# A weight decoder's last step: one VectorE pass for the low bits, where a VectorE shift and a GpSimd addition stood

## The chip, the core and the metric

The kernel runs on one core of a Trainium2 chip. The core has a tensor engine (TensorE, PE in the profile, with its weight loads as PEld), a vector engine (VectorE, DVE), a scalar engine (ScalarE, ACT), GpSimd (POOL), and a queue (SyncE, SP) that starts most of the transfers. The engines work through their own instructions in order and wait for each other by semaphores. The metric is the device time in microseconds, the median of the runs.

## What is computed

Attention of 4 sequences of 576 tokens with 8 heads of 64, half of the heads with a window of 32 tokens, half with a window of 128 in which only every fourth token counts; then two feed-forward layers over all 2304 tokens. The weights of the layers come in as float64.

```
x   = attention(q, k, v)                    # [2304, 512]
xn  = x / sqrt(mean(x * x) + 1e-6) * rms_g
g   = xn @ w_gate                           # [512, 1536]
x   = (silu(g) * (xn @ w_val)) @ w_out      # [1536, 512]
h   = x @ w_in                              # [512, 2048]
out = (max(h, 0) + alpha * min(h, 0)) @ w_out2
```

## The kernel before

**Operands.** Every operand of a large product is a pair of float16 numbers, hi and lo, of the operand times a power of two found on the chip; a product is hi·hi + hi·lo + lo·hi.

**Weights.** They come in 68 blocks of 128 x 512 numbers: gate, val and out of the 12 chunks of the first layer, then in and out of the 16 chunks of the second. On chip they live in `wb`, 70 slots of 2 KB a partition. A block takes two slots as it lands (float64, that is 512 pairs of int32 words), one as float32, one as hi and lo. A block goes through these steps:

- `load_w` (L195): a transfer of 512 KB, issued on SP.
- `decode_w` (L197 to L207): the float64 bits become float32 bits. L202 (VectorE) shifts the high word left by 3 and masks it; L203 (VectorE) puts the two top bits back, with a mask and an or; L204 (VectorE) shifts the low word right by 29, in place, which leaves 3 bits; L205 (GpSimd) adds them to the result as integers. The two landing slots are then free for another load.
- `norm_w`: Gram products on TensorE, or a square on ScalarE (L294), from which the power of two for a group of blocks follows through L256, L310, L313 and L318 to L321 on VectorE.
- `split_w` (L377 to L388): hi on ScalarE (L382); lo on VectorE (L387), or for every third or second block on ScalarE and GpSimd (L384, L385).

**Attention.** The first 128 tokens of the sequences and some later groups are done in float32 with slots of `wb` as their buffers: L585 loads, L595 turns, scores with L541 to L549, L621 turns, L556 to L561 weigh the values, L691 to L693 norm x, L705 to L707 turn it for the first layer.

**Order.** The Python code writes the work down in one sequence, in which the attention's steps, the decoding (`pump`) and the products of the layers are interleaved by a planner that counts slots and products, not time. From that sequence a scheduler with a timeline of its own sorts the instructions of each engine; each engine then works through its list in that order.

Of the kernel before, what the change touches and what calls it, by code (L numbers as in the profile page):

```python
# [22 lines left out]
# Every operand of a large product is carried as a pair of float16 numbers, hi + lo, of the  # L23
# operand times a power of two that is found on the chip so that nothing overflows; a product
# is hi*hi + hi*lo + lo*hi, accumulated in float32, and the powers of two are taken out again.
# The weights come as the bits of float64 numbers and are made float32 on the chip.
# [3 lines left out]
def kernel(  # L30
# [54 lines left out]
    # q: hi, lo, lo, hi and k: hi, lo of each head; rows that a group has no query for hold old ones  # L85
# [27 lines left out]
    def band(m, rows, cols, c0, lo, hi, off=0):  # L113
        # keeps m[p, c0 + c] where lo <= c - (p - off) <= hi
        view = m[0:rows, c0:c0 + cols]
        nc.gpsimd.affine_select(
            out=view, in_=view, compare_op=ALU.is_ge, fill=NEG,
            base=off - lo, pattern=[[1, cols]], channel_multiplier=-1,
        )
        nc.gpsimd.affine_select(  # L120
            out=view, in_=view, compare_op=ALU.is_ge, fill=NEG,
            base=hi - off, pattern=[[-1, cols]], channel_multiplier=1,
        )

    def constants():
        nc.vector.memset(ident, 0.0)
        nc.gpsimd.affine_select(
            out=ident, in_=ident, compare_op=ALU.not_equal, fill=1.0,
            base=0, pattern=[[-1, 128]], channel_multiplier=1,
        )  # L130
        nc.vector.memset(ones_1, 1.0)
        nc.vector.memset(eps, 1e-30)
        nc.gpsimd.memset(qkhl, 0.0)
        nc.vector.memset(mhalf, -0.5)
        for m in (m_spp, m_norm, m_tail):
            nc.vector.memset(m, BIG)
        band(m_spp, 128, 128, 0, -31, 0)
        # m_spd: 0 <= p - c and p % 4 == c % 4
        et = wk.tile([4, 32, 4], BF16, tag="st", bufs=2, name="et")
        nc.vector.memset(et, 0.0)  # L140
        nc.gpsimd.affine_select(
            out=et, in_=et, compare_op=ALU.not_equal, fill=1.0,
            base=0, pattern=[[0, 32], [-1, 4]], channel_multiplier=1,
        )
        same = psw()[:, 0:128]
        mm(same, et.rearrange("p a c -> p (a c)"), et.rearrange("p a c -> p (a c)"), True, True)
        nc.vector.tensor_scalar(m_spd, same, BIG, NEG, ALU.mult, ALU.add)
        band(m_spd, 128, 128, 0, -127, 0)
        band(m_norm, 96, 128, 0, 1, 32)
        for r in range(2):  # L150
            view = m_tail[:, 48 * r:48 * r + 48]
            band(m_tail, 32, 48, 48 * r, 1, 32, 16 * r)
            nc.gpsimd.affine_select(
                out=view, in_=view, compare_op=ALU.is_ge, fill=NEG,
                base=-16 if r else 15, pattern=[[0, 48]], channel_multiplier=1 if r else -1,
            )

# [1 line left out]
    # A block (512 numbers a partition) is two slots of 2 KB as it comes, one as float32 and  # L159
    # one as hi | lo.  # L160
# [12 lines left out]
    def one_slot():  # L173
        # the one that has been free for the longest
        i = min((i for i in range(NSLOT) if free[i]), key=lambda i: (given_back[i], i))
        free[i] = False
        return i
# [19 lines left out]
    def decode_w(b):  # L197
# [6 lines left out]
        nc.vector.tensor_scalar(r[:, :, 0], r[:, :, 0], 29, None, ALU.logical_shift_right)  # L204
        nc.gpsimd.tensor_tensor(w, w, r[:, :, 0], ALU.add)  # L205
# [18 lines left out]
    # Bounds of the squares of the columns' norms: the largest entry of W^T W (bfloat16 heads of  # L224
    # the entries). The scales of gate and val are those of a few blocks each, as the first
    # products begin before all of the weights are there; out's scales take the differences out.
# [18 lines left out]
    def gram(blocks, sums, dst):  # L245
        # blocks of [k, f]: each one's own columns, or the sums over all of them
# [35 lines left out]
    def norm_w(b):  # L282
# [7 lines left out]
        else:  # L290
            # sums of squares, on the engine that waits least then
# [14 lines left out]
    def over_partitions(src, n, dst):  # L306
        # the largest of the partitions' src[:, i], on every partition
# [7 lines left out]
    def root_scale(p, sg, rc):  # L315
        # p: bounds of squares. sg = 2^n with sqrt(p) sg < 2^15; rc = 1 / sg
        ri, si = rc.bitcast(I32), sg.bitcast(I32)
        nc.vector.tensor_scalar(ri, p.bitcast(I32), 1, EXPO, ALU.logical_shift_right, ALU.bitwise_and)  # L318
        nc.vector.tensor_scalar(si, ri, EXPO, None, ALU.bitwise_xor)
        nc.vector.tensor_scalar(sg, sg, 2.0 ** -51, None, ALU.mult)  # L320
        nc.vector.tensor_scalar(rc, rc, 2.0 ** 50, None, ALU.mult)  # L321

    # scales: gate and val of each chunk, out of each, in2, out2
# [9 lines left out]
    def scale_g():  # L333
        # sx with |x / rms * g| sx < 2^15, as |x / rms| <= sqrt(512)
# [8 lines left out]
    def scale_wo():  # L343
        # S with |out| S / (gate's scale * val's) < 2^15 in every chunk
# [12 lines left out]
        # what the last products carry: 2^-60 / (1/sx^2 * 1/S * 1/si * 1/sp)  # L357
# [33 lines left out]
    # The first 128 tokens of the sequences, the next 384 of each, and what is left of them.  # L391
# [61 lines left out]
    # the groups up to this one are float32 products  # L453
# [32 lines left out]
    def a_split_hi(i):  # L486
# [9 lines left out]
        # sc: 0:3 the scales of q, k, v; 3:6 their inverses by 2^50; 6 that of the scores  # L496
# [37 lines left out]
    def softmax(g, scores, scale):  # L534
        # scores: (in PSUM, their heads); leaves exp(s - max) in g["s"] and its sums in g["dn"]
# [16 lines left out]
    def weigh(g, ps, scale):  # L552
        # ps: the weighted values; x = ps / (sum + 1e-9)
# [14 lines left out]
    # The first 128 tokens of the sequences: float32 products, as the tensor engine waits for  # L568
    # weights then; the tiles are slots of the weights that are not yet there.
# [34 lines left out]
    def f_score(i):  # L604
        g = groups[i]
        nq, nk, qk = g["nq"], g["nk"], g["qk"]
        # products of different rows of the array go to different banks
# [108 lines left out]
    # Steps: (what goes before the products of a slot, block or None)  # L716
# [268 lines left out]
    # by when the steps up to the n-th have to be out  # L985
# [4 lines left out]
    def take(d):  # L990
        """The attention's steps that go with this slot."""
# [26 lines left out]
    def pump(n):  # L1018
        # n blocks of weights made float32, and loads of more
# [46 lines left out]
    # the first block's attention, and the weights of the first products as they come  # L1066
# [72 lines left out]
```

## Time and profile before

| | |
|---|---|
| median of 3 runs | 1027.07 us (1027.04 to 1027.49) |
| span of the profiled execution | 1026.5 us |
| TensorE busy | 937.2 us, 91% of the span |
| VectorE busy | 575.6 us, 56% |
| ScalarE busy | 559.9 us, 55% |
| GpSimd busy | 377.8 us, 37% |
| GpSimd's additions of L205 | 68, 100.3 us |

The shares are means over stages that differ: the weights are loaded and decoded in the first 300 us, and the rest of the run is products with what is then on chip. So the rows below are cut by stretches of time. A busy engine may be one whose instruction is held up; for that the length of an instruction is compared with that of its like elsewhere.

### The profile page before, as it was taken

Reading aid. Unit: us, or ns where it says so; the run is one execution under the profiler, and the core shown is the slowest. Engines: PE = TensorE matmul, PEld = TensorE weight load, DVE = VectorE, ACT = ScalarE, POOL = GpSimd, SP = SyncE. Lnnn points to the kernel's source line nnn. Section 1 sums busy time; section 2 is a strip of 40 time slices with the busy share of each in tenths; the row PEclk is TensorE's granted clock in tenths of the full one; section 3 lists DMA queues with packets and bytes.
Section 4 is the critical chain, followed back from the end, with each engine's and each line's share of the span. In section 5 each row is a group of like instructions: output and inputs, shape, how many; then the busy total and the mean of one; then the engine's idle time right before and its main releaser. Section 6 shows DMA issues by size and latency. Waiting matters only on the chain.

```text
span 1026.5 us, 17830 instructions
## 1 busy us (share of the span) xinstructions
PE 937.2 (91%) x6270; PEld 583.3 (57%) x6270; DVE 575.6 (56%) x1396; ACT 559.9 (55%) x1604; POOL 377.8 (37%) x394
## 2 busy tenths in 40 slices
PE   5454879988889989999999999999999999999997
PEld 3444765566545656665555555555555555765564
DVE  5999986787888766564445575434352111331111
ACT  3142657554669988777655677644454312333343
POOL 3564645345534454533232333322142211122222
PEclk9676889999899999999999999999999999999999
DMA  9991323643454354344344353331120000101000
GB/s 255 299 338 45 101 72 102 160 118 102 146 110 96 64 96 93 80 97 99 67 106 64 85 117 80 79 84 38 38 43 6 29 16 1 32 1 21 1 31 21
DMA packets 191608, 88.06 MB, mean 86 GB/s; under 512 B 176800, under 2 KB 180384, under 8 KB 191520
## 3 DMA queue, kind: packets, MB, share of 16 engines
q1 hardware_dynamic: 188896, 82.22, 33.0%
q10 hardware_dynamic: 2624, 4.72, 1.4%
q8 instruction: 49, 0.80, 0.3%
q14 instruction: 39, 0.32, 0.1%
HBM read 55.32 MB, written 6.55 MB: 60 GB/s over the span
## 4 chain that ended last, share of the span: by engine, by line
PE 68%; DVE 18%; DMA 6%; ACT 4%; issue 2%; POOL 1%; SPq 1%; ACTq 0%; DVEq 0%; POOLq 0%
PE psw L92 40%; PE acc L92 27%; DVE wb L203 3%; DVE wb L204 3%; DVE wb L202 2%; DMA wb<-in_moe_w_in_dram 2%; DVE wb L387 2%; DMA wb<-in_moe_w_out_dram 1%; DVE wb L693 1%; DVE wb L541 1%; DMA rkv<-in_v_dram 1%; DMA qkT<-qkhl 1%; DVE dn L556 1%; ACT wb L549 1%; POOL wb L205 1%
## 5 line engine op out<-in xcount | busy, mean ns | idle before, releaser
L92 PE MATMUL psw<-xy,wb 128*128 128x384 f16 (+1 forms) x3360 | 530.3, 307 | 5.2 <-DVE t L875 2.7
L92 PEld LDWEIGHTS <-wb 128*128 128x128 f16 (+1 forms) x4014 | 390.4, 100 | 247.5 <-issue 13.4
L92 PE MATMUL acc<-wb,hl 128*128 128x512 f16 x1002 | 246.2, 381 | 4.9 <-ACT hl L877 1.2
L932 DVE SCALAR_TENSOR_TENSOR p<-m,nal,p 128x384 f32<-128x384 f32 (+1 forms) x112 | 71.4, 638 | 166.6 <-ACT p L931 166.0
L92 PEld LDWEIGHTS <-hl 128*128 128x128 f16 x1002 | 96.0, 98 | 98.8 <-issue 3.4
L205 POOL TENSOR_TENSOR wb<-wb 128x512 int32<-128x512 int32 x68 | 100.3, 1482 | 94.5 <-DVE wb L203 61.8
L92 PE MATMUL acc<-wb 128*128 128x512 f16 x510 | 124.0, 379 | 0.7 <-ACT wb L934 0.6
L883 POOL TENSOR_TENSOR hl<-p,hl 128x384 f16<-128x384 f32 (+1 forms) x74 | 61.3, 828 | 116.4 <-ACT hl L934 103.9
L883 POOL TENSOR_TENSOR hl<-t,hl 128x384 f16<-128x384 f32 (+1 forms) x56 | 51.1, 912 | 129.6 <-ACT hl L877 129.6
L874 DVE SCALAR_TENSOR_TENSOR t<-t,psw 128x384 f32<-128x384 f32 (+1 forms) x84 | 41.2, 490 | 79.9 <-ACT t L873 79.7
L930 ACT ACTIVATE m<-psw 128x384 f32<-128x384 f32 (+1 forms) x112 | 48.6, 434 | 65.9 <-PE psw L92 65.1
L873 ACT ACTIVATE t<-psw,tsc 128x384 f32<-128x384 f32 (+1 forms) x84 | 44.1, 525 | 71.9 <-PE psw L92 62.7
L92 PE MATMUL psw<-wb 128*128 128x128 bf16 (+6 forms) x448 | 57.3, 301 | 10.7 <-POOL wb L205 8.4
L659 POOL TENSOR_TENSOR phl<-s,phl 96x512 f16<-96x512 f32 (+2 forms) x33 | 36.8, 1114 | 70.0 <-ACT phl L653 40.5
L382 ACT ACTIVATE wb<-wb,wsg 128x512 f16<-128x512 f32 x68 | 46.6, 711 | 27.3 <-DVE wrc L321 18.7
L875 DVE SCALAR_TENSOR_TENSOR t<-t,psw 128x384 f32<-128x384 f32 (+1 forms) x84 | 41.2, 490 | 27.8 <-PE psw L92 26.5
L549 ACT ACTIVATE s<-s,mx 96x128 f32<-96x128 f32 (+2 forms) x132 | 50.1, 381 | 10.9 <-DVE mx L546 10.7
L883 POOL TENSOR_TENSOR wb<-p,wb 128x384 f16<-128x384 f32 (+1 forms) x38 | 32.0, 842 | 63.5 <-ACT wb L934 57.5
L203 DVE SCALAR_TENSOR_TENSOR wb<-wb 128x512 int32<-128x512 int32 x68 | 54.7, 810 | 0.2
L883 POOL TENSOR_TENSOR wb<-t,wb 128x256 f16<-128x256 f32 (+1 forms) x28 | 24.1, 861 | 80.2 <-ACT wb L877 72.1
L877 ACT ACTIVATE hl<-t 128x384 f16<-128x384 f32 (+1 forms) x56 | 26.8, 479 | 44.4 <-DVE t L875 44.4
L934 ACT ACTIVATE hl<-p 128x384 f16<-128x384 f32 (+1 forms) x74 | 34.6, 467 | 28.9 <-DVE p L932 28.8
(160 smaller groups left out, 1154.2 us busy)
## 6 DMA issues: line engine op xcount, KB each, us to landing
wb<-in_moe_w_out_dram SPq DMA_DIRECT2D x28, 512.0 KB, 4.4
wb<-in_moe_w_in_dram SPq DMA_DIRECT2D x16, 512.0 KB, 3.6
wb<-in_moe_w_gate_dram SPq DMA_DIRECT2D x12, 512.0 KB, 7.7
wb<-in_moe_w_val_dram SPq DMA_DIRECT2D x12, 512.0 KB, 7.3
out_dram<-o ACTq DMA_DIRECT2D x16, 256.0 KB, 2.5
rkv<-in_k_dram SPq DMA_DIRECT2D x23, 128.0 KB, 2.7
rkv<-in_v_dram SPq DMA_DIRECT2D x23, 128.0 KB, 2.8
rq<-in_q_dram SPq DMA_DIRECT2D x23, 96.0 KB, 2.1
```

Source lines behind the costliest of these rows:

```text
L92: nc.tensor.matmul(o, a, b, start=start, stop=stop)
L203: nc.vector.scalar_tensor_tensor(w, r[:, :, 1], -0x40000000, w, ALU.bitwise_and, ALU.bitwise_or)
L205: nc.gpsimd.tensor_tensor(w, w, r[:, :, 0], ALU.add)
L382: nc.scalar.activation(half(b, 0), dec(b), ACTF.Copy, scale=wsg[:, s:s + 1])
L549: nc.scalar.activation(s[:nq, h, :nk], s[:nq, h, :nk], ACTF.Exp, bias=mx[:nq, 1, h:h + 1], accum_out=g["dn"][:nq, h])
L659: nc.gpsimd.tensor_tensor(phl[:nq, 1, :, :nk], g["s"][:nq, :, :nk], phl[:nq, 0, :, :nk], ALU.subtract)
L873: nc.scalar.activation(t[:, :T], pg[:, :T], ACTF.Tanh, scale=tsc[:, chunk(c):chunk(c) + 1])
L874: nc.vector.scalar_tensor_tensor(t[:, :T], t[:, :T], 1.0, pg[:, :T], ALU.add, ALU.mult)
L875: nc.vector.scalar_tensor_tensor(t[:, :T], t[:, :T], 2.0 ** -46, pv[:, :T], ALU.mult, ALU.mult)
L883: nc.gpsimd.tensor_tensor(a[:, 1, :T], t[:, :T], a[:, 0, :T], ALU.subtract)
L930: nc.scalar.activation(m[:, :T], ps[:, :T], ACTF.Relu, scale=-(2.0 ** -15))
L932: nc.vector.scalar_tensor_tensor(p[:, :T], m[:, :T], nal[:, c:c + 1], p[:, :T], ALU.mult, ALU.add)
```

## The change

L204 and L205 become one VectorE instruction that shifts the low word right by 29 and puts the result into `w` with an or (the three low bits of `w` are zero then, so or and plus are the same). The low word is no longer written back. The diff also takes comments out; the lines keep their numbers up to 203, and what follows `decode_w` stands one line higher: L541 is L540, L693 is L692, L707 is L706.

```diff
         nc.vector.tensor_scalar(w, r[:, :, 1], 3, 0x3FFFFFFF, ALU.logical_shift_left, ALU.bitwise_and)
         nc.vector.scalar_tensor_tensor(w, r[:, :, 1], -0x40000000, w, ALU.bitwise_and, ALU.bitwise_or)
-        nc.vector.tensor_scalar(r[:, :, 0], r[:, :, 0], 29, None, ALU.logical_shift_right)
-        nc.gpsimd.tensor_tensor(w, w, r[:, :, 0], ALU.add)
+        nc.vector.scalar_tensor_tensor(w, r[:, :, 0], 29, w, ALU.logical_shift_right, ALU.bitwise_or)
         give(i, i + 1)
```

The scheduler sorts all engines anew for it. VectorE's list at its first decoded blocks, before:

```order
L202 TENSOR_SCALAR wb<-wb 128x512
L204 TENSOR_SCALAR wb<-wb 128x512
L203 SCALAR_TENSOR_TENSOR wb<-wb 128x512
L147 TENSOR_SCALAR m_spd<-psw 128x128
L202 TENSOR_SCALAR wb<-wb 128x512
L204 TENSOR_SCALAR wb<-wb 128x512
L203 SCALAR_TENSOR_TENSOR wb<-wb 128x512
```

The same place now:

```order
L202 TENSOR_SCALAR wb<-wb 128x512
L203 SCALAR_TENSOR_TENSOR wb<-wb 128x512
L147 TENSOR_SCALAR m_spd<-psw 128x128
L204 SCALAR_TENSOR_TENSOR wb<-wb 128x512
L202 TENSOR_SCALAR wb<-wb 128x512
L203 SCALAR_TENSOR_TENSOR wb<-wb 128x512
L204 SCALAR_TENSOR_TENSOR wb<-wb 128x512
```

The number of VectorE instructions is the same; the third of a block comes last now and has two tensor inputs. On the same engine, where the first scales are there (`wsg`), the second group's x is normed (`ms` and `gs` are its inputs) and turned (`xy_73` is the first layer's input), and the first blocks are split, before:

```order
L280 TENSOR_SCALAR tsc<-xsc,wrc 128x1
L204 TENSOR_SCALAR wb<-wb 128x512
L387 SCALAR_TENSOR_TENSOR wb<-wb,wsg 128x512 x2
L693 SCALAR_TENSOR_TENSOR wb<-wb,ms,gs 128x512
L202 TENSOR_SCALAR wb<-wb 128x512
L387 SCALAR_TENSOR_TENSOR wb<-wb,wsg 128x512
L202 TENSOR_SCALAR wb<-wb 128x512
L387 SCALAR_TENSOR_TENSOR wb<-wb,wsg 128x512
L204 TENSOR_SCALAR wb<-wb 128x512
L203 SCALAR_TENSOR_TENSOR wb<-wb 128x512
L202 TENSOR_SCALAR wb<-wb 128x512
L203 SCALAR_TENSOR_TENSOR wb<-wb 128x512
```

and now:

```order
L279 TENSOR_SCALAR tsc<-xsc,wrc 128x1
L692 SCALAR_TENSOR_TENSOR wb<-wb,ms,gs 128x512
L204 SCALAR_TENSOR_TENSOR wb<-wb 128x512
L386 SCALAR_TENSOR_TENSOR wb<-wb,wsg 128x512 x2
L204 SCALAR_TENSOR_TENSOR wb<-wb 128x512
L386 SCALAR_TENSOR_TENSOR wb<-wb,wsg 128x512 x2
L202 TENSOR_SCALAR wb<-wb 128x512 x3
L706 TENSOR_TENSOR xy_73<-psw,xy_73 128x4x128
L202 TENSOR_SCALAR wb<-wb 128x512
L203 SCALAR_TENSOR_TENSOR wb<-wb 128x512 x3
```

The norm has moved ahead of the first splits, and the shifts of the next blocks stand together behind them. On GpSimd, around the last normed x of the float32 groups (`ms`), among the splits of the first layer's results (`hl`), before:

```order
L883 TENSOR_TENSOR hl_108<-t,hl_108 128x256
L205 TENSOR_TENSOR wb<-wb 128x512
L692 TENSOR_TENSOR ms<-ms,mhalf 96x1
L205 TENSOR_TENSOR wb<-wb 128x512 x3
L883 TENSOR_TENSOR hl_109<-t,hl_109 128x256
L205 TENSOR_TENSOR wb<-wb 128x512 x3
L883 TENSOR_TENSOR hl_110<-t,hl_110 128x256
```

and now:

```order
L691 TENSOR_TENSOR ms<-ms,mhalf 96x1
L882 TENSOR_TENSOR hl_110<-t,hl_110 128x256
L882 TENSOR_TENSOR hl_107<-t,hl_107 128x256
L882 TENSOR_TENSOR hl_108<-t,hl_108 128x256
L691 TENSOR_TENSOR ms<-ms,mhalf 96x1
L882 TENSOR_TENSOR hl_109<-t,hl_109 128x256
L882 TENSOR_TENSOR hl_110<-t,hl_110 128x256
```

The additions are gone and the rest keeps its order.

## Rows read from the trace of the kernel before

**Rows 1.** the page's slices (40 of 25.7 us, tenths of busy time): VectorE
```profile
DVE  5999986787888766564445575434352111331111
```

**Rows 2.** busy time by stretch (us; count), granted clock, DMA share, GB/s
```profile
25.00:61.00 36.00, 11.20 (x66) 10.47 (x67) 36.00 (x67) 9.97 (x24) 21.56 (x15) 0.64 0.98 314
61.00:135.00 74.00, 51.36 (x381) 42.75 (x381) 73.86 (x139) 31.96 (x81) 40.84 (x32) 0.78 0.38 130
135.00:300.00 165.00, 146.10 (x1027) 98.39 (x1028) 131.85 (x302) 98.87 (x311) 78.44 (x66) 0.94 0.45 121
300.00:1027.00 727.00, 714.10 (x4738) 422.77 (x4735) 320.29 (x845) 410.16 (x1158) 226.72 (x258) 1.00 0.27 56
```

**Rows 3.** chain of waits, 25 to 135 us, shares by line
```profile
by line: DVE wb L203 20.8%; DVE wb L204 19.4%; DVE wb L202 13.4%; DVE wb L387 12.5%; DVE dn L556 5.3%; DVE wb L693 4.2%; issue 3.7%; DVE nrm L256 3.5%; DVE wb L541 2.5%; DVE wb L561 2.2%; DVE t L874 2.1%; DVE mx L545 1.7%; DVE diag L310 1.6
```

**Rows 4.** TensorE's waits, 25 to 300 us: us in total, times, longest
```profile
PE psw L705 <- DVE wb L693: 28.6, 5, 15.6
PE psw L92 <- DVE diag L310: 15.2, 3, 8.4
PE psw L92 <- POOL wb L205: 8.4, 2, 6.2
```

**Rows 5.** groups, VectorE, 25 to 135 us (count, busy us, mean ns, idle)
```profile
L203 DVE SCALAR_TENSOR_TENSOR wb<-wb 128x512 int32<-128x512 int32 x30 | 25.5, 855 | 0.0
L204 DVE TENSOR_SCALAR wb<-wb 128x512 int32<-128x512 int32 x38 | 24.6, 650 | 0.0
L202 DVE TENSOR_SCALAR wb<-wb 128x512 int32<-128x512 int32 x30 | 18.1, 609 | 0.0
L387 DVE SCALAR_TENSOR_TENSOR wb<-wb,wsg 128x512 f16<-128x512 f32 x15 | 15.3, 1028 | 0.0
L556 DVE TENSOR_SCALAR dn<-dn 128x4 f32<-128x4 f32 x5 | 6.3, 1255 | 0.0
L693 DVE SCALAR_TENSOR_TENSOR wb<-wb,ms,gs 128x512 f32<-128x512 f32 x4 | 4.9, 1220 | 0.0
```

**Rows 6.** groups, VectorE, 0 to 25 us
```profile
L203 DVE SCALAR_TENSOR_TENSOR wb<-wb 128x512 int32<-128x512 int32 x4 | 2.7, 682 | 0.0
...
L204 DVE TENSOR_SCALAR wb<-wb 128x512 int32<-128x512 int32 x4 | 1.7, 428 | 0.0
...
L556 DVE TENSOR_SCALAR dn<-dn 128x4 f32<-128x4 f32 x3 | 0.5, 166 | 0.1
```

**Rows 7.** timeline, VectorE: start us, us, what
```profile
31.95 1.40 DVE L202 TENSOR_SCALAR wb<-wb 128x512 int32<-128x512 int32 x1
...
34.87 1.50 DVE L204 TENSOR_SCALAR wb<-wb 128x512 int32<-128x512 int32 x1
...
61.03 0.74 DVE L387 SCALAR_TENSOR_TENSOR wb<-wb,wsg 128x512 f16<-128x512 f32 x1
...
69.76 1.29 DVE L202 TENSOR_SCALAR wb<-wb 128x512 int32<-128x512 int32 x1
...
254.47 4.22 DVE L693 SCALAR_TENSOR_TENSOR wb<-wb,ms,gs 96x512 f32<-96x512 f32 x1 [1.34 <-POOL ms L692]
```

**Rows 8.** timeline, GpSimd
```profile
31.77 1.29 POOL L205 TENSOR_TENSOR wb<-wb 128x512 int32<-128x512 int32 x1 [0.63 <-DVE wb L203]
34.69 1.39 POOL L205 TENSOR_TENSOR wb<-wb 128x512 int32<-128x512 int32 x1 [1.63 <-DVE wb L203]
...
254.40 3.74 POOL L205 TENSOR_TENSOR wb<-wb 128x512 int32<-128x512 int32 x3
```

**Rows 9.** groups, GpSimd, 25 to 135 us
```profile
L205 POOL TENSOR_TENSOR wb<-wb 128x512 int32<-128x512 int32 x30 | 44.9, 1506 | 41.0 <-DVE wb L203 27.6 <-issue 6.7 <-ACT wb L384 4.3
```

**Rows 10.** timeline, SP
```profile
51.09 0.92 SPq L195 DMA_DIRECT2D wb<-in_moe_w_val_dram  x2
```

**Rows 11.** the page's transfers: count, KB, median us to landing
```profile
wb<-in_moe_w_val_dram SPq DMA_DIRECT2D x12, 512.0 KB, 7.3
```

**Rows 12.** chain of waits, 135 to 300 us, shares by line
```profile
by line: PE psw L92 17.5%; DMA wb<-in_moe_w_in_dram 10.1%; DMA wb<-in_moe_w_out_dram 7.6%; DVE wb L203 6.6%; issue 6.4%; DVE wb L202 5.9%; PE acc L92 5.3%; POOL wb L205 4.3%; DVE wb L693 3.4%; DVE wb L204 3.4%; DMA qkT<-qkhl 3.1%; ACT wb L5
```

## The prediction

> **What bounds the kernel now.** The page's slices come first [rows 1]: VectorE stands at 7 to 9 tenths from the second slice to the eighth and falls off slowly. Cut into stages [rows 2], the run has three. From 25 to 135 us (stage A) VectorE is busy 36.00 of 36 and 73.86 of 74 us, TensorE 11.20 and 51.36, at a mean granted clock of 0.64 and 0.78 of its full level. From 135 to 300 us (stage B) TensorE is busy 146.10 of 165 us and VectorE 131.85. After 300 us (stage C) TensorE is busy 714.10 of 727 us: what is late there is the products. The chain of waits in stage A [rows 3] is VectorE nearly throughout, and its three largest lines are the decoding of the weights: L203 20.8%, L204 19.4%, L202 13.4%. TensorE's waits up to 300 us are for VectorE's results (the normed x of L693, the diagonal of L310) and twice for the GpSimd addition itself [rows 4]. So stage A is worth what VectorE's queue is worth, microsecond for microsecond, as long as nothing else is late.
>
> Busy does not mean working there. The same lines have two lengths: before 25 us, where GpSimd and VectorE seldom meet, a shift of L204 takes 428 ns, a pass of L203 682 ns and the small L556 166 ns [rows 6]; from 25 to 135 us they take 650, 855 and 1255 ns on average [rows 5]. The timeline shows why [rows 7, 8]: the shift that begins at 31.95 takes 1.40 us and the one at 34.87 takes 1.50 us, and both last until just after the end of a GpSimd addition of L205, which began 0.18 us ahead of each (31.77 plus 1.29, 34.69 plus 1.39).
>
> **The change part by part.** Each of the 68 blocks loses one VectorE shift and one GpSimd addition and gets one VectorE pass with two tensor inputs.
>
> The new pass: the trace has no shift-and-or of this line, but L203 is the same operation on the same operands (a strided int32 input, w as second input and output, 512 elements), so I take its undisturbed 682 ns. Against the shift of 428 ns that is 0.254 us more a block [rows 6]. Stage A decodes 30 blocks (30 additions [rows 9], 30 of L203): 30 x 0.254 = 7.6 us more, all on VectorE's path. Bounds: 0 if the longer pass fills gaps (there are none, so I exclude it), and a doubled pass below, as a rival.
>
> The addition that goes: while it runs VectorE is held. Over the undisturbed lengths, stage A holds 30 x (855 - 682) = 5.2 us on L203, 38 x (650 - 428) = 8.4 on L204, 30 x (609 - 428) = 5.4 on L202, 5 x (1255 - 166) = 5.4 on L556, and against the 0.74 us of the row at 61.03 [rows 7] 15 x (1028 - 740) = 4.3 on L387 and 4 x (1220 - 740) = 1.9 on L693 [rows 5]: 30.6 us. Not all of it is L205's, since GpSimd also splits weights and activations then. L205 is 44.9 us [rows 9] of GpSimd's 21.56 + 40.84 = 62.4 us [rows 2], 72%, which gives 22 us. The upper end is all of it, 30.6 us, about 1.0 us for each of the 30 additions, and that is what the two pairs of [rows 7, 8] show (1.40 and 1.50 against about 0.42). I take 26 us, between them. Stage A: -26 + 7.6 = -18.4 us, with bounds of -22 + 7.6 = -14.4 and -30.6 + 7.6 = -23.0.
>
> The Trainium skill (SBUF — State Buffer, "Who interferes with whom") calls the port that VectorE and GpSimd share an exclusive lock: whoever starts first has it for its whole instruction, and the other is blocked, not slowed. By it an addition could cost VectorE up to its whole length of about 1.28 us, an estimate of 38 us for the 30; stage A would then be -31 us and the whole -36 us, 991 us. The rows stop at 30.6 us, as an addition often begins under an instruction that is already running.
>
> What could eat it in stage A is the loads. The 20th block's load is issued at 51.09 us; its first shift starts at 69.76 [rows 7, 10], and VectorE never waited for a load in this stage (idle 0.0 in [rows 5]). With a landing time of 7.3 us for such a block (the median of its like, [rows 11]) it is there by about 58.4, 11 us early. By then VectorE is ahead by some 18.4 x (70 - 25)/110 = 7.5 us. The cover holds with 3 or 4 us left. TensorE has 110 - 62.6 = 47 us of idle time in stage A to give.
>
> The order: the scheduler sorts anew. A block is now three passes in a row on VectorE where the addition went to the other queue, and the second normed x and its four first splits stand a few rows earlier. On TensorE 48 products of the first layer stand ahead of the second set of Gram products, before as after. So I price the order at nothing, with 3 us to either side in the range.
>
> Stage B: the decoding of the other 34 blocks. Here TensorE is the busiest, and the chain [rows 12] gives L205 4.3% of 165 us = 7.1 us and L204 3.4% = 5.6 us, which at stage A's mean of 650 ns [rows 5] is some 8.6 shifts, each 0.254 us longer: +2.2 us. Net -4.9 us. That is in keeping with the largest single wait: at 254.47 a normed x takes 4.22 us under three additions in a row [rows 7, 8], 3.5 us over 0.74, and TensorE's L705 stands behind it (a part of the 28.6 us of [rows 4]). Bounds: a gain of at most the 18.9 us that TensorE idles in the stage, and I go no further than -8; a loss of 34 x 0.254 = 8.6 us if every new pass were late and nothing came back, of which I keep 0 as the upper end, since the held time is seen here too. Stage C has no decoding: 0.
>
> **Sum.** -18.4 - 4.9 = -23.3 us. The profiled execution's span is 1026.5 us, 0.6 us under the median of 1027.07, so the median falls to about 1004 us.
>
> **The rivals.** (1) *Slower, because a full engine gets more work.* If the stretched lengths in stage A are not GpSimd's doing, or its other operations take the place that the additions leave, the new pass is a pure cost: +7.6 us in stage A and +2.2 in B, 1037 us. It decides when less than 7.6 of the 30.6 us goes away, 0.25 us an addition. Against it speak the ends of the stretched shifts, which follow the ends of the additions. For it the Trainium skill (Perfetto Trace Analysis, "Optimizing Scalar/DVE Operations") says that work may be taken off a saturated VectorE, to GpSimd too, though it adds that the two share a port, so that it might not help; here the first half would speak against this change, and the trace sides with the second.
> (2) *Something else is late.* Loads, TensorE at its lower clock (0.64 to 0.78 in stage A), or ScalarE takes over after half of stage A's gain, and stage B gives back nothing: -9 us, 1018 us. For it: the load cover is thin and the order of a few hundred instructions has moved. Against it: TensorE's 47 idle us.
> (3) *More*, if each addition holds VectorE for about its length, and the chain in stage B shortens by its upper end: -23 - 8 = -31 us, 996 us. The lock rule of the Trainium skill (SBUF — State Buffer), cited above, leans this way.
> (4) *The pass isn't what it seems.* If shift-and-or runs at half of L203's rate, 1.36 us, it costs 0.936 us over the shift: +28.1 - 26 = +2 us in stage A, and -7.1 + 8.0 = +0.9 in stage B, 1030 us. Nothing in the trace hints at it; L203 has a mask and an or, and the old L204 a shift, at the lengths of their kinds.
>
> **How the numbers follow.** Forecast 0.68, (1) 0.05, (2) 0.14, (3) 0.09, (4) 0.04. The forecast's own spread is -14.4 - 0 + 3 to -23 - 4.9 - 3, some 996 to 1016. Half of (2) and half of (3) are taken in for 8 in 10: 995 to 1018. A measurement of this kernel tells about 0.2%, 2 us, from no change. Faster 0.88 (the forecast, (3) and most of (2)), same 0.03 (a little of (2) and of the two bad cases), slower 0.09.
>
> **What would show it.** Right: from 25 us until the first layer runs freely VectorE's L202 and L203 near 0.43 and 0.69 us instead of 0.61 and 0.86; the new pass near 0.7; TensorE's long waits for L693 and L310 shorter, and the end of stage A at about 117 instead of 135 us; a span short by that and a little more. Wrong: the passes as long as before with GpSimd idle (1), VectorE idle before L202 for loads (2), or a new pass of over 1 us (4).

## The result, and the profile after

| | before | after |
|---|---|---|
| median | 1027.05 us (1025.52 to 1027.49) | 992.32 us (991.9 to 992.97) |
| ratio | | 0.9672, 95% interval 0.9658 to 0.9686 |
| span of the profiled execution | 1026.5 us | 990.8 us |
| TensorE busy | 937.2 us | 927.5 us |
| VectorE busy | 575.6 us | 546.4 us |
| GpSimd busy | 377.8 us | 285.9 us |

The change is a gain of 3.3%, 34.7 us of the median and 35.7 us of the span: in the foretold direction, but half as much again as the forecast's 23.3 us, and 2.7 us below the lower end of the range.

To see where it came from, the stages are cut by events instead of by the clock: stage A from 25 us to the end of the fourth normed x (L693 before, L692 after), stage B from there to the end of the last decoding pass (the last L203), stage C the rest. Up to 25 us the two traces are nearly alike. The columns of the first fence are those of [rows 2]; this is the kernel before by its own stage ends.

```profile
25.00:135.30 110.30, 62.56 (x446) 53.22 (x446) 110.16 (x206) 41.92 (x105) 62.39 (x47) 0.73 0.58 190
135.30:295.70 160.40, 141.80 (x1002) 96.04 (x1003) 128.86 (x295) 94.87 (x297) 75.16 (x63) 0.94 0.45 123
295.70:1026.50 730.80, 718.40 (x4763) 425.12 (x4761) 322.98 (x850) 414.17 (x1173) 230.00 (x261) 1.00 0.27 56
```

The same view of the changed kernel:

```profile
25.00:118.80 93.80, 58.78 (x451) 51.42 (x449) 91.03 (x208) 42.68 (x107) 21.79 (x18) 0.80 0.68 225
118.80:256.50 137.70, 135.53 (x1008) 93.77 (x1009) 118.31 (x298) 92.32 (x292) 29.55 (x30) 0.97 0.52 143
256.50:990.80 734.30, 719.23 (x4757) 424.81 (x4754) 322.99 (x852) 415.07 (x1176) 229.21 (x259) 1.00 0.27 56
```

Stage A is 16.5 us shorter, stage B 22.7, and stage C 3.5 us longer: 35.7 us. In both A and B the numbers of instructions (in brackets) agree closely, so nearly the same work is compared, with one exception that matters for the split. Stage A of the kernel before decodes 30 blocks but runs 38 of the shifts of L204 [rows 5]: eight of them belong to blocks of stage B. The new pass cannot stand ahead of its block's L203, so the changed kernel runs 30 in stage A and the others in stage B. L204 in stage B, before (135 to 300 us) and then after (119 to 257 us):

```profile
L204 DVE TENSOR_SCALAR wb<-wb 128x512 int32<-128x512 int32 x26 | 13.8, 530 | 16.8 <-DMA wb<-in_moe_w_out_dram 10.1 <-DMA wb<-in_moe_w_in_dram 6.5
...
L204 DVE SCALAR_TENSOR_TENSOR wb<-wb 128x512 int32<-128x512 int32 x34 | 24.5, 724 | 0.0
```

So some 8 x 0.428 = 3.4 us of stage A's gain (an estimate from the undisturbed length of a shift [rows 6]) is work that moved into stage B. VectorE is busy 19.1 us less in A and 10.6 us less in B, although it has the longer passes. In stage B TensorE, with 1008 products instead of 1002, is busy 6.3 us less, at a granted clock of 0.97 instead of 0.94 of its full level, and its time without work falls from 18.6 to 2.2 us.

The lengths answer to [rows 5]: VectorE's groups of the changed kernel from 25 to 135 us (count, busy us, mean ns, idle before them).

```profile
L203 DVE SCALAR_TENSOR_TENSOR wb<-wb 128x512 int32<-128x512 int32 x33 | 23.8, 730 | 0.0
L204 DVE SCALAR_TENSOR_TENSOR wb<-wb 128x512 int32<-128x512 int32 x33 | 23.4, 712 | 0.0
L386 DVE SCALAR_TENSOR_TENSOR wb<-wb,wsg 128x512 f16<-128x512 f32 x16 | 14.8, 938 | 0.8 <-ACT wb L381 0.8
L202 DVE TENSOR_SCALAR wb<-wb 128x512 int32<-128x512 int32 x33 | 14.7, 454 | 0.0
...
L692 DVE SCALAR_TENSOR_TENSOR wb<-wb,ms,gs 128x512 f32<-128x512 f32 x4 | 3.0, 743 | 0.3 <-POOL ms L691 0.3
...
L555 DVE TENSOR_SCALAR dn<-dn 128x4 f32<-128x4 f32 x6 | 1.4, 242 | 0.0
```

L203 falls from 855 to 730 ns, L202 from 609 to 454, the norm from 1220 to 743, the small L555 (L556 before) from 1255 to 242. The new pass takes 712 ns; over the whole run its median is 679 ns, against 680 of L203. TensorE's waits, to be laid beside [rows 4], here from 25 us to the end of stage B (us in total, times, longest):

```profile
PE psw L704 <- DVE wb L692: 18.6, 4, 10.0
PE psw L92 <- DVE diag L309: 8.2, 3, 4.7
PE psw L92 <- DVE wb L204: 6.6, 1, 6.6
```

28.6 us for the normed x are 18.6 now, 15.2 for the diagonal 8.2, and the 8.4 us for GpSimd's addition have become one wait of 6.6 for the new pass. And the chain of waits of stage A, 25 to 118.8 us, which answers to [rows 3]:

```profile
by line: DVE wb L203 13.5%; DVE wb L204 10.8%; DVE wb L386 10.7%; DMA wb<-in_q_dram 10.1%; PE psw L92 8.6%; DVE wb L202 8.2%; DMA wb<-in_moe_w_gate_dram 8.1%; issue 6.3%; DMA rkv<-in_v_dram 4.1%; DVE nrm L255 3.6%; DVE t L874 3.0%; DVE t L8
```

The decoding has 32.5% of the chain where it had 53.6%, and loads, which were not among the large lines before, have 22.3%: stage A is no longer VectorE alone.

### The profile page after: what moved, and what is told of

Its sections match the earlier page's. It is cut to its first block, busy times and chain, and to the rows that moved or that the text cites. A ratio compares the mean times of both kernels' runs of the same rounds, so it can differ in the third digit from the quotient of the medians.

```text
span 990.8 us, 17722 instructions
## 1 busy us (share of the span) xinstructions
PE 927.5 (94%) x6270; PEld 579.0 (58%) x6270; DVE 546.4 (55%) x1396; ACT 558.7 (56%) x1604; POOL 285.9 (29%) x326
## 4 chain that ended last, share of the span: by engine, by line
PE 69%; DVE 13%; DMA 7%; ACT 4%; issue 4%; SPq 2%; POOL 1%; DVEq 0%; ACTq 0%; POOLq 0%
PE psw L92 40%; PE acc L92 28%; DVE wb L203 3%; DVE wb L204 2%; DMA wb<-in_q_dram 2%; DVE wb L202 2%; DVE wb L386 1%; DMA rkv<-in_v_dram 1%; ACT s L548 1%; DMA wb<-in_moe_w_gate_dram 1%; DVE t L874 1%; SPq L584 1%; ACT wb L381 1%; DMA wb<-in_moe_w_out_dram 1%; DVE t L873 1%
## 5 line engine op out<-in xcount | busy, mean ns | idle before, releaser
L931 DVE SCALAR_TENSOR_TENSOR p<-m,nal,p 128x384 f32<-128x384 f32 (+1 forms) x112 | 68.1, 608 | 161.8 <-ACT p L930 160.8
L929 ACT ACTIVATE m<-psw 128x384 f32<-128x384 f32 (+1 forms) x112 | 48.6, 434 | 66.3 <-PE psw L92 64.8
L92 PE MATMUL psw<-wb 128*128 128x128 bf16 (+6 forms) x448 | 55.0, 294 | 9.3 <-DVE wb L204 6.6
L882 POOL TENSOR_TENSOR wb<-t,wb 128x256 f16<-128x256 f32 (+1 forms) x28 | 23.7, 847 | 109.9 <-ACT wb L876 101.7
L384 POOL TENSOR_TENSOR wb<-wb 128x512 f16<-128x512 f32 x28 | 37.4, 1337 | 46.5 <-ACT wb L383 36.7
L933 ACT ACTIVATE hl<-p 128x384 f16<-128x384 f32 (+1 forms) x74 | 34.5, 466 | 27.7 <-DVE p L931 27.6
L930 ACT ACTIVATE p<-psw 128x384 f32<-128x384 f32 (+1 forms) x112 | 48.7, 435 | 0.0
L204 DVE SCALAR_TENSOR_TENSOR wb<-wb 128x512 int32<-128x512 int32 x68 | 48.6, 718 | 0.1
```

Of the source, the lines that this page charges most:

```text
L92: nc.tensor.matmul(o, a, b, start=start, stop=stop)
L204: nc.vector.scalar_tensor_tensor(w, r[:, :, 0], 29, w, ALU.logical_shift_right, ALU.bitwise_or)
L384: nc.gpsimd.tensor_tensor(half(b, 1), dec(b), half(b, 0), ALU.subtract)
L882: nc.gpsimd.tensor_tensor(a[:, 1, :T], t[:, :T], a[:, 0, :T], ALU.subtract)
L929: nc.scalar.activation(m[:, :T], ps[:, :T], ACTF.Relu, scale=-(2.0 ** -15))
L930: nc.scalar.activation(p[:, :T], ps[:, :T], ACTF.Relu, scale=2.0 ** -15)
```

## The experiments

The theory: the gain is the time for which GpSimd's additions hold VectorE, less the longer pass. The rivals: the *result* of the addition was late (a wait, not a hold); the new order of the instructions did it; waits for loads went away; or stage B gained only through stage A. Three of the kernels (the idle addition, the idle memset, the late additions) do work on top that nobody uses. The stages in the table are cut as above; "VectorE" is its busy time over the run by the page, "idle B" its idle time in stage B.

| kernel | median us | ratio to before (95%) | stage A | stage B | VectorE | idle B |
|---|---|---|---|---|---|---|
| before | 1027.05 | 1 | 110.3 | 160.4 | 575.6 | 31.5 |
| after | 992.32 | 0.9672 (0.9658, 0.9686) | 93.8 | 137.7 | 546.4 | 19.4 |
| idle addition | 1040.78 | 1.0145 (1.0127, 1.0164) | 119.1 | 164.9 | 595.0 | 23.2 |
| idle memset | 1026.34 | 1.0003 (0.999, 1.0017) | 100.0 | 167.5 | 580.4 | 28.6 |
| early blocks only | 1009.52 | 0.9841 (0.9822, 0.9859) | 98.1 | 153.2 | 558.4 | 27.0 |
| late blocks only | 1003.93 | 0.9782 (0.9761, 0.9804) | 106.8 | 139.1 | 560.9 | 20.8 |
| or as a pass of its own | 1011.45 | 0.986 (0.9842, 0.9878) | 106.1 | 146.2 | 569.9 | 19.3 |
| the same, shift not ahead | 1011.11 | 0.9834 (0.9806, 0.9861) | 101.3 | 156.1 | 573.9 | 23.1 |
| before, shift not ahead | 1025.43 | 0.9983 (0.9971, 0.9995) | 108.2 | 158.3 | 572.4 | 26.8 |
| before, other order | 1024.34 | 0.9983 (0.9969, 0.9997) | 109.9 | 156.8 | 573.5 | 27.9 |
| after, other order | 990.78 | 0.9659 (0.9637, 0.968) | 90.0 | 140.5 | 549.0 | 20.6 |
| after, no GpSimd splits | 989.14 | 0.9646 (0.9619, 0.9673) | 93.2 | 140.0 | 549.8 | 21.1 |
| both of the last two | 985.44 | 0.9605 (0.9583, 0.9627) | 91.7 | 139.8 | 555.0 | 20.8 |
| after, late additions | 990.29 | 0.965 (0.9625, 0.9675) | 94.3 | 137.9 | 557.6 | 19.7 |

### The hold without the wait: an idle addition

The changed kernel, and behind its new pass the old addition as far as GpSimd is concerned: it reads the result and the low word and writes the low word. No engine waits for its result; the two landing slots come free behind it, as before.

```diff
         nc.vector.scalar_tensor_tensor(w, r[:, :, 0], 29, w, ALU.logical_shift_right, ALU.bitwise_or)
+        nc.gpsimd.tensor_tensor(r[:, :, 0], w, r[:, :, 0], ALU.add)
```

> The changed kernel with a GpSimd integer addition of the old size put back behind the fused pass: it reads w and the low word and writes the low word, which nobody reads (the landing slots come free behind it, as before). No engine waits for its result. If GpSimd's additions cost by holding VectorE and by filling GpSimd's queue, most of the gain goes again: VectorE's passes near 0.6 to 0.85 us in the first 135 us and a time of 1025 to 1040 us (the fused pass is 0.25 us longer than the old shift). If they cost because someone waits for their result, the time stays at 992 to 998 us.

1040.78 us, just above the upper end of the first range: 48.5 us over the changed kernel, 0.71 us for each of the 68 additions, and 15.1 us over the kernel before of the same runs (1025.7 us), a little less than the 17.3 us that 68 passes, each 0.254 us longer, add up to. Its groups from 25 to 135 us, VectorE, then GpSimd:

```profile
L204 DVE SCALAR_TENSOR_TENSOR wb<-wb 128x512 int32<-128x512 int32 x28 | 29.5, 1057 | 0.0
L203 DVE SCALAR_TENSOR_TENSOR wb<-wb 128x512 int32<-128x512 int32 x29 | 24.4, 850 | 0.0
L202 DVE TENSOR_SCALAR wb<-wb 128x512 int32<-128x512 int32 x29 | 18.9, 664 | 0.0
...
L205 POOL TENSOR_TENSOR wb<-wb 128x512 int32<-128x512 int32 x28 | 44.3, 1586 | 45.5 <-DVE wb L204 24.3 <-issue 10.1 <-DMA wb<-in_moe_w_gate_dram 5.4
```

The stretched lengths of [rows 5] are back with an addition for which no result waits: L203 850 ns (855 before), L202 664 (609). So the cost of the addition was not that its result was late. VectorE's busy time says the same: 595.0 - 546.4 = 48.6 us for 48.5 us of time. (Whether that wait was worth anything at all is not shown: the 2.2 us between 17.3 and 15.1 are near what another order moves, 1.5 us below.) Nor is it the slots that come free later: in stage B VectorE waits 3.6 us for the loads of weights here, and 2.7 us in the changed kernel.

### Stage A's blocks and stage B's

The new pass for the first 32 blocks only, and for the other 36 only; the rest as before.

```diff
-        nc.vector.scalar_tensor_tensor(w, r[:, :, 0], 29, w, ALU.logical_shift_right, ALU.bitwise_or)
+        if n_done[0] < 32:
+            nc.vector.scalar_tensor_tensor(w, r[:, :, 0], 29, w, ALU.logical_shift_right, ALU.bitwise_or)
+        else:
+            nc.vector.tensor_scalar(r[:, :, 0], r[:, :, 0], 29, None, ALU.logical_shift_right)
+            nc.gpsimd.tensor_tensor(w, w, r[:, :, 0], ALU.add)
```

> The first 32 blocks decoded with the fused pass, the other 36 with the old shift and GpSimd addition. If the two stages gain separately, this has the gain of the first 135 us alone, 16 to 18 us: 1009 to 1011 us. If the later gain (some 19 us between 135 and 300 us) only follows from the earlier start of the first layer, it is near 992 us.

> The reverse: the first 32 blocks with shift and GpSimd addition, the other 36 with the fused pass. If the additions of the second stage cost some 19 us by themselves: 1007 to 1010 us. If the second stage gains only because the first one does, 1020 to 1027 us.

The early blocks alone gain 16.2 us, as foretold, the late ones alone 21.8, more than foretold, against 1025.7 us. That is 0.51 and 0.61 us a block. The late blocks need no help from the early ones: their gain is in stage B (139.1 us, nearly the changed kernel's 137.7). Stage A is 106.8 us with them, 3.5 us shorter than before, though its own 30 blocks are decoded as before; it has 30 low-word steps instead of 38, and the eight shifts that left it (3.4 us) would account for that. Apart they make 38.0 us, together 34.7, so the halves overlap a little. That stage B gains only what stage A hands on has fallen.

### What a microsecond of VectorE is worth

The old shift and a VectorE or as its own pass, without GpSimd.

```diff
-        nc.gpsimd.tensor_tensor(w, w, r[:, :, 0], ALU.add)
+        nc.vector.tensor_tensor(w, w, r[:, :, 0], ALU.bitwise_or)
```

> Shift and or as two VectorE instructions in place of the fused one, nothing on GpSimd. Against the changed kernel VectorE has one more shift of 0.33 us a block (start to start). If VectorE's own work sets the first stage, +10 us there (30 x 0.33) and little in the second: 1000 to 1005 us, still 20 us or more under the kernel before. If only GpSimd mattered, 992 to 995 us.

1011.45 us: 14.3 us better than the kernel before in the same runs (1025.7 us), although VectorE has 68 more instructions, but 19.1 us behind the changed kernel, more than I expected. VectorE's groups from 25 to 135 us:

```profile
L205 DVE TENSOR_TENSOR wb<-wb 128x512 int32<-128x512 int32 x32 | 23.1, 724 | 0.0
L203 DVE SCALAR_TENSOR_TENSOR wb<-wb 128x512 int32<-128x512 int32 x32 | 21.5, 680 | 0.0
L204 DVE TENSOR_SCALAR wb<-wb 128x512 int32<-128x512 int32 x39 | 18.0, 461 | 1.8 <-DMA wb<-in_moe_w_out_dram 1.0 <-DMA wb<-in_moe_w_in_dram 0.8
L202 DVE TENSOR_SCALAR wb<-wb 128x512 int32<-128x512 int32 x31 | 13.3, 443 | 0.0
```

The passes are at their short lengths, so the rest is the pass itself. VectorE is busy 23.5 us longer than in the changed kernel and the time is 19.1 us longer: 0.81 of it arrives at the end. In the two spans stage A is 12.3 us longer (with 38 shifts again, eight of them for stage B's blocks), stage B 8.5, and stage C 3.3 shorter. So VectorE sets the pace in stage B too, though TensorE is the busier engine there. My error in the expectation was to let only stage A pay.

### Loads and the place of the shift

In the kernel before, the scheduler puts the shift of the low word up to 9 blocks ahead of its block (nine other blocks' L203 stand between), most of all around the middle of the weights; in the changed kernel no pass can go ahead of L203. In stage B of the kernel before VectorE waits for loads at the head of its list (VectorE's longest waits, 135.3 to 295.7 us; us in total, times, longest):

```profile
DVE wb L204 <- DMA wb<-in_moe_w_out_dram: 10.1, 6, 3.8
DVE wb L204 <- DMA wb<-in_moe_w_in_dram: 6.5, 4, 2.9
DVE dn L556 <- ACT wb L549: 3.4, 4, 1.4
DVE t L874 <- ACT t L873: 3.4, 4, 2.2
```

With 0.8 us before L202 that is 17.4 us; in the changed kernel such waits are 2.7 us in all. So it looked as if 14 us of the gain were the new place of the shift. The test is to bind the shift behind L203 without any other change: it writes over the high word, which L203 must have read, and the addition reads it there. This was done to the kernel before, and to the one with the or as a pass.

```diff
-        nc.vector.tensor_scalar(r[:, :, 0], r[:, :, 0], 29, None, ALU.logical_shift_right)
-        nc.gpsimd.tensor_tensor(w, w, r[:, :, 0], ALU.add)
+        nc.vector.tensor_scalar(r[:, :, 1], r[:, :, 0], 29, None, ALU.logical_shift_right)
+        nc.gpsimd.tensor_tensor(w, w, r[:, :, 1], ALU.add)
```

> The kernel before with its four steps, but the low word's shift writes over the high word (the addition reads it there), so that it cannot be put ahead of its block's L203 any more; in the kernel before it stands up to 10 blocks ahead of its block in the weights' second half, and VectorE waits there 17.4 us for loads at its head (L204 behind DMA, 135 to 296 us). Theory A (these waits are part of what the change gave back): the load waits fall to some 3 to 4 us as in the kernel with an idle addition, VectorE's idle time in that stage from 31.5 to about 23, the first stage stays at 110 us, and the whole takes 1015 to 1020 us. Theory B (the waits are filled by others as soon as they go, only the hold of VectorE by GpSimd counts): 1023 to 1028 us, like before. Theory C (held back shifts make the additions and thus the freed slots late): over 1029 us.

> The shift and a VectorE or in two passes, no GpSimd addition, the shift again bound behind its block's L203. With shifts ahead of their blocks this form took 1011.45 us, with 10.3 us of load waits in 131 to 277 us but no more idle time of VectorE in all (19.3 us) than the changed kernel (19.4). Theory A (load waits cost by themselves): 1002 to 1006 us, load waits at some 3 us. Theory B (they are filled by others): 1009 to 1013 us. What then remains over the changed kernel's 992.3 us is the extra pass alone, some 23.5 us of VectorE's busy time.

1025.43 us against 1026.97 of before in the same runs, and 1011.11 against the 1011.45 of its own form: theory B. (Those two forms ran beside different runs of the kernel before; by their ratios to it they differ by 2.6 us, 0.9834 to 0.986, and the intervals overlap.) The longest of VectorE's waits in stage B (133.2 to 291.5 us) of the first:

```profile
DVE dn L556 <- ACT wb L549: 5.6, 4, 2.3
DVE t L874 <- ACT t L873: 5.3, 4, 2.4
DVE xd L561 <- PE psw L92: 2.8, 2, 1.5
DVE ss L908 <- ACT yhl L907: 1.9, 2, 1.5
DVE dn L556 <- ACT s L549: 1.7, 1, 1.7
DVE wb L202 <- DMA wb<-in_moe_w_in_dram: 1.4, 1, 1.4
```

The waits for loads are down from 17.4 to 2.1 us, and waits for ScalarE and TensorE stand in their place; the stage is 158.3 us instead of 160.4. (In the second the stages trade some microseconds with each other, 101.3 and 156.1 us, so of it only the whole is compared.) The 17.4 us of load waits, the most striking idle time of stage B, were worth some 1.5 us there.

### Only the order

`OFF` is the lead that the attention's steps have with the scheduler. Another value gives VectorE and the others another order of the same instructions, in the changed kernel and in the one before.

```diff
-    OFF = 400
+    OFF = 100
```

> The changed kernel with the attention's steps written at another priority (100 in place of 400), so that the scheduler sorts all engines otherwise; the work is the same. If the gain is the work and the hold, 988 to 998 us. If it came from a lucky order, 1005 us or more.

> The kernel before with the same other priority. If the hold sets its time, 1020 to 1035 us; if its order was unlucky, it comes down to 1010 us or less.

1.5 us less in either case (990.78 us instead of 992.32 after, 1024.34 instead of 1025.82 before). The difference between before and after is 33.6 us in this order too. An order can be worth a microsecond or two; it does not carry the result.

### A GpSimd instruction that only writes

In the changed kernel GpSimd fills, once a block, three quarters of the landing slots, which have been read by then, with zeros: about as long as an addition, but with nothing read.

```diff
         nc.vector.scalar_tensor_tensor(w, r[:, :, 0], 29, w, ALU.logical_shift_right, ALU.bitwise_or)
+        nc.gpsimd.memset(wb16[:, i * 1024:i * 1024 + 1536], 0.0)
```

> The changed kernel with a GpSimd operation of about the same length (1.4 us) per block that only writes: zeros into the landing slots and the slot behind is not touched (1536 half words of the 2048 of the pair), after the last pass has read them. GpSimd's queue and the slots are as late as with an addition. If it is the occupied queue or the late slots that cost, 1030 to 1040 us; if it is the hold of VectorE by GpSimd's reading, 992 to 1000 us; a hold by writing too gives 1030 to 1040 us with VectorE's passes stretched again, which the lengths of L202 and L203 tell.

1026.34 us, between the two ranges that I had written down: 34 us over the changed kernel, and level with the kernel before. VectorE's groups from 25 to 135 us, then GpSimd's:

```profile
L203 DVE SCALAR_TENSOR_TENSOR wb<-wb 128x512 int32<-128x512 int32 x32 | 23.1, 735 | 0.0
L202 DVE TENSOR_SCALAR wb<-wb 128x512 int32<-128x512 int32 x32 | 22.7, 723 | 0.0
L204 DVE SCALAR_TENSOR_TENSOR wb<-wb 128x512 int32<-128x512 int32 x32 | 22.3, 708 | 0.0
...
L556 DVE TENSOR_SCALAR dn<-dn 128x4 f32<-128x4 f32 x5 | 4.0, 793 | 0.4 <-ACT wb L549 0.4
...
L557 DVE RECIPROCAL dn<-dn 128x4 f32<-128x4 f32 x6 | 1.0, 167 | 0.0
...
L205 POOL MEMSET wb<- 128x1536 f16 x31 | 43.3, 1413 | 38.8 <-DVE wb L204 25.6 <-issue 10.6 <-DVE ms L691 1.5
```

Stretched are the TENSOR_SCALAR instructions, which have one tensor input: L202 723 ns (454 in the changed kernel), L556 793 (242). Of the five of L556 three start under a memset; they take 0.94, 0.32 and 1.91 us and end 0.02 to 0.04 us behind the end of one. The passes with two tensor inputs are not stretched: 735 and 708, against 730 and 712. With the addition, which reads, both kinds were. One input alone does not decide it: the reciprocal of L557, with the same 128 x 4 numbers, keeps its 167 ns (169 in the changed kernel). Two lines of this kernel's timeline on VectorE and GpSimd show one hold (start us, us):

```profile
38.53 1.38 POOL L205 MEMSET wb<- 128x1536 f16 x1 [2.55 <-DVE wb L204]
...
38.73 1.46 DVE L202 TENSOR_SCALAR wb<-wb 128x512 int32<-128x512 int32 x1
```

The shift that starts 0.20 us behind the memset ends 0.28 us behind its end, at 40.19 us. The Trainium skill (SBUF — State Buffer, "Who interferes with whom") says that a VectorE instruction with two SBUF inputs meets GpSimd only where GpSimd reads, while one in a mode that takes both pairs of ports meets any, and that whoever starts first blocks the other for its whole instruction. The rows agree with the first half (735 and 708 ns beside a memset that only writes), and with the second if the shift of L202 is in such a mode; that it has the shorter undisturbed length of the two (0.42 us to 0.68) fits, but no view here shows the mode.

The slots are freed late in this kernel, behind the memset, but little of the 34 us can be that: VectorE's waits for loads of weights in stage B are 4.4 us (2.7 in the changed kernel), and its busy time grew by 34.0 us.

### GpSimd's other work, and the fastest version

GpSimd's share of the splits of weights (L383, L384) also holds VectorE, by 5.3 us in stage A of the changed kernel. There they were given to VectorE, 28 passes; and then this and the other order together.

```diff
-    LO1, LO2 = 3, 2
+    LO1, LO2 = 1000, 1000
```

> The changed kernel with all low halves of the split weights on VectorE (the 28 subtractions of GpSimd and their second ScalarE pass gone). In the changed kernel these subtractions still hold VectorE for some 8 us up to the end of the decoding (12 of them), and VectorE's own pass is 0.66 us: 12 x 0.66 = 8 us. If a microsecond of VectorE is worth about one of the end there, whether it works or is held, the time stays at 990 to 995 us. If GpSimd's work costs more than its hold, 985 to 990 us.

> The changed kernel with both edits that came out a little lower: all low halves of the weights on VectorE, and the other priority of the attention's steps. If what is left is GpSimd's hold before the end of the decoding, 986 to 990 us. If the two edits only move the same slack about, 989 to 993 us.

989.14 us and, with `OFF = 100`, 985.44 us (ratio 0.9605 of before, 6.9 us below the changed kernel): the best version found, faster than both. VectorE's 28 passes more are not free, its busy time is 3.4 us longer, but ScalarE is busy 15.5 us less (543.2 to 558.7) and GpSimd 31.1 (254.8 to 285.9). The gain over the changed kernel is in stage C (728.2 instead of 734.3 us), not in the decoding: stage B is 2.3 us longer. So the 3.2 us of the first is no further evidence for the hold.

### The same hold where TensorE is late

The changed kernel with 48 additions of 128 x 512 on a tile that nobody needs any more, in the second layer, beside L931 on VectorE.

```diff
+        if kind == "B" and j >= 4:
+            qi = qkhl.bitcast(I32)[:, 0:512]
+            nc.gpsimd.tensor_tensor(qi, qi, qi, ALU.add)
```

> The changed kernel with 48 GpSimd integer additions of the old size (128x512 int32) on a tile that nobody needs any more, put into the second layer's last three token blocks, behind the decoding. There TensorE is busy nearly all the time and VectorE idles more than half of it. If a hold costs only where VectorE is late, 992 to 995 us, with VectorE's passes there stretched. If GpSimd's additions cost wherever they stand (0.7 us each, as where the weights are decoded), 1020 to 1027 us.

990.29 us, a little under the first range and not slower than the changed kernel (992.32). From 700 to 990 us, L931 on VectorE and the additions on GpSimd (L1099):

```profile
L931 DVE SCALAR_TENSOR_TENSOR p<-m,nal,p 128x384 f32<-128x384 f32 x32 | 27.9, 873 | 68.6 <-ACT p L930 68.6
...
L1099 POOL TENSOR_TENSOR qkhl<-qkhl 128x512 int32<-128x512 int32 x48 | 53.0, 1104 | 4.2 <-DVE x L560 2.1
```

The changed kernel has, for the same stretch:

```profile
L931 DVE SCALAR_TENSOR_TENSOR p<-m,nal,p 128x384 f32<-128x384 f32 x32 | 20.1, 627 | 79.0 <-ACT p L930 79.0
```

VectorE is held here too (873 ns instead of 627), and its idle time before L931 shrinks by 10.4 us in exchange. The hold costs where VectorE sets the pace, and nothing where it waits for others.

## Why the prediction was right in direction and short in size

**The bound and the hold: right.** VectorE's queue was stage A's end, and its long instructions were instructions held up. Counted for each stretched VectorE instruction against the GpSimd operation that it lay under, with the shortest tenth of its form as its undisturbed length, L205 held VectorE 27.0 us in stage A; the forecast took 26. All holds together fell from 34.5 to 7.3 us there. The idle addition shows the cause, and not only the coincidence.

**The new pass: right.** 0.254 us more a block was taken from L203's 682 ns against the shift's 428; the pass has a median of 679 ns. Rival 4 (a pass at half the rate) is out, and rival 1 (a pure cost) with it: with the addition left in place, the pass does cost its price (15.1 of 17.3 us), so rival 1 named the right price for a case that did not occur.

**Stage A: right in its main term, and near in the sum partly by luck.** -18.4 us foretold, with bounds of -14.4 and -23.0; -16.5 measured. The longer passes were priced as 30 x 0.254 = +7.6 us, but 38 shifts left the stage and 30 passes came: by the same lengths 30 x 0.682 - 38 x 0.428 = +4.2 us. Against that ten other VectorE instructions, some 3 us, fell into the shorter stage A, and idle time rose by 2.6 us (0.1 to 2.8 us), 2.1 of it waits for TensorE. These three were not in the sum and come to some +2 us together (-3.4, +3 and +2.6). VectorE's busy time fell by 19.1 us. The end of the stage was foretold at about 117 us and came at 118.8; L203 at 0.69 and L202 at 0.43 us came at 0.73 and 0.45. The cover of the loads held: L202 waited for none in stage A (idle 0.0 in its row above).

**Stage B: wrong, and this is the term that failed.** -4.9 us foretold, with a hand-set end at -8; -22.7 measured. The step was to read what the addition is worth from its own share of the chain, 4.3% [rows 12]. That share is the time in which something waited for the addition's result. It does not contain the hold, which shows in the chain under the names of the held: L203, L202, the norm. Counted as in stage A, over 135.3 to 295.7 us L205 holds VectorE for 19.6 us, not 7.1. The longer passes were mis-sized too, at +2.2 us: 34 passes came for 26 shifts, 34 x 0.682 - 26 x 0.428 = +12.1 us. The net of the two is -7.5 us; VectorE's busy time fell by 10.6, part of it because three instructions (1.5 us) now run in stage A. The wait at 254.47 us [rows 7], which the forecast cited as the largest single wait, was one of 18 holds.

The other half of stage B, and the larger part of what the sum missed, is idle time of VectorE, 31.5 to 19.4 us, with no term in the sum at all. The forecast went by TensorE as the busiest engine there, where VectorE sets the pace too: an extra pass on VectorE makes stage B 8.5 us longer (the or as a pass of its own). The two kernels with the shift held back show that it is not the load waits, which exchange for other waits. It follows the hold only roughly: 19.3 to 23.1 us in the kernels of the table that decode stage B's blocks without GpSimd, 23.2 to 31.5 in those that run an addition or a memset there. That a held VectorE delays ScalarE and TensorE, for which it then waits itself, would fit; it was argued and not shown. TensorE's side of the same 22.7 us is 16.4 us less without work and 6.3 us less at work, at the higher granted clock; how much of the one follows from the other stays open too.

**The limit of -8.** TensorE's 18.9 us without work were named as the most that stage B could give, and then not used. Even that bound was not one: the products themselves took 6.3 us less while the granted clock of the stage rose from 0.94 to 0.97.

**Order at nothing: right.** 1.5 us for another order in both kernels, and 1.5 and 0.3 for the shift's place (2.6 by the ratios in the second), within the 3 us allowed. That holds for the time; between the stages the new order moved the eight shifts.

**Stage C at nothing:** it is 3.5 us longer. Over the kernels of the table that leave stage C's work alone it lies between 729.5 and 734.3 us, the changed kernel at its upper end. Why, was not tried.

**Rival 2** (something else late, 1018 us) did not come, though loads now have 22.3% of stage A's chain. **Rival 3** (996 us) came nearest, and the estimate from the lock rule of the Trainium skill (SBUF — State Buffer, "Who interferes with whom"), 991 us, nearer still, but by other sums: the estimate had -31 us in stage A, where -16.5 was measured, and little in stage B. An addition cost 0.71 us of time in the idle-addition kernel, not its whole 1.28 us.

## What to carry to other kernels

Where VectorE's instructions have two lengths and the long ones end with GpSimd's, price a GpSimd operation by what it holds in every stage in which VectorE sets the pace, the stage of a busier TensorE included, and not by its own share of the chain. Moving that work to VectorE, in a pass that replaces another one, can then shorten VectorE's own busy time. In stage B here the net of that price (7.5 us) is a third of the gain (22.7 us), and why VectorE's idle time fell as well stays open. When a step can no longer run ahead of its block, count its instructions by stage before and after. A long wait in a list of waits is no price either, until something shows what would be late next.

## What the hardware showed that was not expected

- A GpSimd operation that writes and does not read stretched VectorE's TENSOR_SCALAR instructions, down to 128 x 4 numbers (793 ns on average instead of 242), and left passes with two tensor inputs (735 ns against 730) and a reciprocal of 128 x 4 numbers (167 against 169) alone.
- Instructions that follow each other on VectorE overlap in the records: of the changed kernel's L203 at 31.81 us the length is 0.66 us, but the next shift starts at 32.38.

```profile
31.81 0.66 DVE L203 SCALAR_TENSOR_TENSOR wb<-wb 128x512 int32<-128x512 int32 x1
32.38 0.42 DVE L202 TENSOR_SCALAR wb<-wb 128x512 int32<-128x512 int32 x1
```

  So an instruction more costs the queue less than its row: the or as a pass of its own adds 461 + 724 - 712 = 473 ns a block by the rows of stage A, but 23.5 us / 68 = 346 ns of busy time.
- A VectorE with 129 of 160 us at work set the pace of a stage in which TensorE was at work for 142: of two busy engines that wait for each other, the less busy one was where time could be had.
